# Exponentials and sines taken channel-major on half batches, with TensorE transposing the results and VectorE multiplying them from PSUM

## The chip, the cores and the metric

The kernel runs on one core of a Trainium2 chip. The metric is the device time of one execution in microseconds, as the median of several runs. An engine is named as the profile names it: PE is TensorE, DVE is VectorE, ACT is ScalarE, POOL is GpSimd, SP is the engine whose queue issues most transfers.

## The reference, cut to what matters

```python
mag = np.sqrt(a_re * a_re + a_im * a_im)
scale = np.minimum(mag, 0.999) / (mag + 1e-06)
a_re_n, a_im_n = (a_re * scale, a_im * scale)
for t in range(S):
    ar, ai = (a_re_n[:, :, t, :, None], a_im_n[:, :, t, :, None])
    new_re = ar * S_re - ai * S_im
    new_im = ar * S_im + ai * S_re
    S_re, S_im = (new_re + k_t v_t^T, new_im)
    y[:, :, t] = q_t^T S_re
```

Batch is 4, heads 8, sequence 768, head dimension 48, so that one token has 384 channels. The attention output then goes through a mixture of experts (top one of 8, 384 to 1024 to 384) and a second stage `((x @ w1) * (x @ w2)) @ w3 @ w_out`, over 3072 tokens, all in float32.

## The kernel before

**The whole.** The recurrence is computed in chunks of 128 tokens. A decay `a` is written as magnitude and angle; running sums of the log magnitude L (restarted at each chunk) and of the angle r (in turns) turn the recurrence into products: q is multiplied by exp(L/2), k by exp(-L/2), and each is taken with cos and sin of the angle. Within a chunk the scores of these products are masked and applied to v; between chunks a state S of 96 x 48 per head is carried. After the 24 chunks come the routing (which token to which expert) and the two dense stages, which are matrix products split into high and low parts.

**Two layouts.** The logs, sums and angles are worked out channel-major: 128 channels on the partitions, three tiles (index `i`) for the 384 channels, tokens along the free dimension. q and k are token-major: 128 tokens on the partitions, 384 channels along the free dimension. `f_mag` (L196) and `f_ang` (L262) do the channel-major part per batch and tile, on 128 x 768 elements, except for the first batch, which is done as two halves of 128 x 384. L and r are then brought into the token layout chunk by chunk: `t_mag` (L294) has PE transpose L into PSUM, ACT take both exponentials from there (`ep`, `em`), POOL multiply q (L304) and DVE multiply k (L305); `t_trig` (L308) does the same for r, with three activations (absolute value, sine, cosine).

**A unit** is one chunk of one batch. `t_prod` (L324) forms the four products K cos, K sin, Q cos, Q sin from SBUF operands; the table `PROD` says which of the four go to POOL (one in batch 0, two in the others), the rest go to DVE. `t_tr` (L339) transposes K and Q, four heads at a time, and copies the result out of PSUM (`kt`, `qt`); the table `EVAC` says on which engine: three of four copies on DVE in batch 0, two of four later. `t_sc` (L377) multiplies `kt` and `qt` to scores and masks them on DVE (L390). `t_y` (L394) forms the output, `t_out` (L416) transposes and stores it, `t_st1` and `t_st2` (L354, L362) update the state.

**The order of the work.** `attention` (L452) writes the program: a start (first half batch, four weight conversions `wo_conv`), then the loop over 24 units. In each unit the steps of `STEPS` are emitted in order; the products of unit i+2 are emitted at the end of unit i. Between the steps are put the preparation of the next batch, at the positions in `PLANS`, and the conversion of 20 blocks of the later weights (`w34_step`: float64 bits to float32 on DVE, L625 to L632, split on ACT and POOL, products on PE). Each engine executes its own instructions in a fixed order and waits by semaphores. ACT's functions lie in two table sets, logarithm and exponential (`setA`) and trigonometric (`setT`); a load (L172) changes between them. PSUM has eight buffers `ps`, one per result.

Of the kernel before, what the change touches and what calls it, by code (L numbers as in the profile page):

```python
# [48 lines left out]
SPAN0 = 2  # L49
# [13 lines left out]
)  # L63
ON_POOL = dict(u="110", add="010", m2="111", rat="111", turn="111", sub="111", qm="1", km="0", u0="011", add0="110", m20="011", rat0="001", turn0="000", sub0="110", qm0="1", km0="0")
STEPS = ["sc0", "kt0", "qt0", "sc1", "st1", "y0", "kt1", "lg", "qt1", "y1", "out", "st2"]
BUFS = dict(q=9, k=8, v=4, ep=3, em=2, sn=4, cs=4, Q=2, K=3, kt=4, qt=3, sts=1, S=2, pt=2, ys=3, lts=1, xr=2, st64=1, st32=3, w3h=2, w3l=1, gate=1, s1=3, s2=3, s3=2)
EXTRA = ("MAN", "OFF", "OFFP", "NR", "AIQ", "WO_A", "WO_B", "W6", "W12", "WH", "PROD", "SMUL", "EVAC", "PTE", "GATE", "ND", "D0", "M_PRE")
MAN = 0
OFF = 0
OFFP = 0  # L70
NR = '0000'
AIQ = 1
WO_A = 0
# [3 lines left out]
WH = '000'  # L77
PROD = ['0001', '0101', '1001', '0101']
SMUL = '0010'
EVAC = ['0010', '0110', '0110', '0110']  # L80
PTE = ['00', '00', '00', '00']
GATE = '01000000001100010100000010000100'
ND = 2
D0 = 19.05
M_PRE = 6
# [12 lines left out]
C_RST = C_REV + E  # L98
C_W = C_RST + S


def make_consts():
    import numpy as np

    c = np.zeros((P, C_W), np.float32)
    i = np.arange(P)
    c[:, C_ID:C_ID + P] = np.eye(P)
    c[:, C_MASK:C_MASK + P] = i[:, None] <= i[None, :]
    c[:, C_IROW:C_IROW + ROWS] = np.arange(ROWS)
    c[:, C_ICOL:C_ICOL + NCOL] = np.arange(NCOL)  # L110
    c[:, C_P1] = i - P
# [5 lines left out]
    c[:, C_RST:C_RST + S] = np.arange(S) % P != 0  # L117
# [10 lines left out]
def setup(ctx, tc, g):  # L128
# [14 lines left out]
    for i in range(NTH):  # L143
        f_load(tc, g, 0, i, 0, 1)
    g.cst = g.cp.tile([P, C_RST], F32, name="cst")
    nc.sync.dma_start(out=g.cst, in_=g.I["consts"][:, 0:C_RST])
    g.rst = g.pf.tile([P, S], F32, name="rst")
    nc.sync.dma_start(out=g.rst, in_=g.I["consts"][:, C_RST:C_W])
# [31 lines left out]
def f_load(tc, g, b, i, h0=0, h1=2):  # L180
    nc = tc.nc
    HS = S // 2
    if h0 == 0:
        g.ar[b, i] = g.pf.tile([P, S], F32, tag="ar", bufs=6, name=f"ar{b}{i}")
        g.ai[b, i] = g.pf.tile([P, S], F32, tag="ai", bufs=6, name=f"ai{b}{i}")
    sl = slice(h0 * HS, h1 * HS)
    nc.sync.dma_start(out=g.ar[b, i][:, sl], in_=g.I["are"][b, i * P:(i + 1) * P, sl])
    (nc.scalar if b == 0 and h0 == 0 and AIQ else nc.sync).dma_start(out=g.ai[b, i][:, sl], in_=g.I["aim"][b, i * P:(i + 1) * P, sl])


def eng(nc, op, b, h0, i):
    m = ON_POOL[op + "0" if b == 0 and h0 == 0 and op + "0" in ON_POOL else op]
    return nc.gpsimd if m[i:i + 1] == "1" else nc.vector


def f_mag(tc, g, b, i, h0=0, h1=2):  # L196
    nc = tc.nc
    pa = g.pf
    V, A = nc.vector, nc.scalar
    HS = S // 2  # L200
    lo, n = h0 * HS, (h1 - h0) * HS
    k = f"{b}{i}{h0}"
    ck = 2 * (2 * (b * NTH + i) + h0)
    t = {}

    def tl(nm, bufs, key):
        return pa.tile([P, S], F32, tag=nm, bufs=bufs, name=f"{key}_{k}")[:, :n]

    def o1():
        t["ar"], t["ai"] = g.ar[b, i][:, lo:lo + n], g.ai[b, i][:, lo:lo + n]  # L210
        t["s1"] = tl("s1", BUFS["s1"], "s1")
        t["s2"] = tl("s2", BUFS["s2"], "s2")
# [3 lines left out]
    def o2():  # L216
        dp = pa.tile([P, S], BF16, tag="dp", bufs=1, name=f"dp_{k}")[:, :n]
        A.activation(dp, t["ar"], AF.Relu, bias=g.hpi[:, 3:4], scale=-1.0, accum_out=g.chk[:, ck:ck + 1])
        A.activation(t["s1"], t["s1"], AF.Square, scale=0.5)
        eng(nc, "m2", b, h0, i).tensor_tensor(t["ar"], t["s1"], t["s2"], ALU.add)  # L220

    def o3():
        dp = pa.tile([P, S], BF16, tag="dp", bufs=1, name=f"dq_{k}")[:, :n]
        A.activation(dp, t["s2"], AF.Relu, bias=g.hpi[:, 2:3], accum_out=g.chk[:, ck + 1:ck + 2])

    def o4():
        tact(tc, g, t["s1"], t["s1"], AF.Ln, scale=4.0)

    def o5():
        tact(tc, g, t["s1"], t["s1"], AF.Exp, scale=-0.5)  # L230
        eng(nc, "rat", b, h0, i).tensor_tensor(t["ai"], t["ai"], t["s1"], ALU.mult)

    def o6():
        tact(tc, g, t["ar"], t["ar"], AF.Ln, scale=4.0)

    def o7():
        tact(tc, g, t["s2"], t["ar"], AF.Exp, bias=g.hpi[:, 1:2], scale=-0.5)
        V.scalar_tensor_tensor(t["s2"], t["ar"], LN999, t["s2"], ALU.min, ALU.subtract)
        V.tensor_tensor_scan(t["ar"], g.rst[:, :n], t["s2"], 0.0, ALU.mult, ALU.add)  # L239
# [66 lines left out]


def t_trig(tc, g, b, c):  # L308
    nc = tc.nc
    A = nc.scalar  # L310
    pa = g.pa
    u = f"{b}{c}"
    pr = g.ps.tile([P, 512], F32, tag="ps", name=f"pr{u}")
    for i in range(NTH):
        nc.tensor.transpose(pr[:, i * P:(i + 1) * P], g.r[b, i][:, c * P:(c + 1) * P], g.ident)
    sn = pa.tile([P, DM], F32, tag="sn", bufs=BUFS["sn"], name=f"sn{u}")
    cs = pa.tile([P, DM], F32, tag="cs", bufs=BUFS["cs"], name=f"cs{u}")
    A.activation(cs, pr[:, :DM], AF.Abs)
    tact(tc, g, sn, pr[:, :DM], AF.Sin, scale=TWO_PI)
# [987 lines left out]
```

## Time and profile before

| | us |
|---|---|
| median of 3 runs (lowest, highest) | 1011.28 (1010.45, 1015.07) |
| span of the profiled execution | 1008.9 |
| start, up to the first masked score (L390) | 0 to 56 |
| the 24 units, up to the last output | 56 to 405 |
| routing, gather and first weights | 405 to 443 |
| dense stages | 443 to 1009 |

The page gives the span of the profiled execution, from its first instruction to its last; what the runs measure has some 2.4 us around it. The mean granted clock of PE over the span is 0.923 of full speed. Busy shares over the whole span (PE 84%, DVE 57%, ACT 38%, POOL 40%) mix stages with different limits; they have to be read by stage.

### The profile page before, as it was taken

To read this page: it belongs to the slowest core of one execution; us is meant where nothing else is said; L and a number is where in the kernel's file an instruction comes from. 1 tells how busy PE (TensorE), PEld (TensorE's weight loads), DVE (VectorE), ACT (ScalarE), POOL (GpSimd) and SP (SyncE) were. 2 spreads that over 40 slices of the span, in tenths; PEclk is the share of its full clock that TensorE was granted. 3 is DMA by queue.
4 is the path that set the end of the run, shared out by engine and by line. 5 is a ranking of instruction groups with operands and counts; after the bars stand their busy time and mean duration, and the time that the engine had idled before them with its cause. 6 is when DMAs were issued, how large, how long until landed. Compare 5 with 4: busy or idle time off the path is not lost.

```text
span 1008.9 us, 14148 instructions
## 1 busy us (share of the span) xinstructions
PE 845.7 (84%) x5539; PEld 798.6 (79%) x5539; DVE 577.7 (57%) x858; ACT 378.7 (38%) x749; POOL 399.3 (40%) x295
## 2 busy tenths in 40 slices
PE   0286668776968798677999999999999999999994
PEld 0175547765857687576999999999999999999993
DVE  6998997899899999866224323224232242232221
ACT  5676557564733533323222222222222222222221
POOL 3556775777467663344016311047030172100101
PEclk9986757988887899879999999999999999999997
DMA  8445225232412443565002300014010030000000
GB/s 294 129 124 168 61 87 169 81 89 86 127 49 66 140 131 118 143 185 173 20 11 77 89 25 26 1 36 139 1 45 1 25 93 17 25 1 1 25 1 26
DMA packets 55037, 78.26 MB, mean 78 GB/s; under 512 B 15462, under 2 KB 43352, under 8 KB 54962
## 3 DMA queue, kind: packets, MB, share of 16 engines
q1 hardware_dynamic: 46322, 66.93, 21.6%
q0 software_dynamic: 5120, 9.70, 3.4%
q10 hardware_dynamic: 3520, 0.64, 0.3%
q8 instruction: 45, 0.74, 0.3%
q14 instruction: 30, 0.25, 0.1%
HBM read 64.57 MB, written 12.87 MB: 77 GB/s over the span
## 4 chain that ended last, share of the span: by engine, by line
PE 41%; DVE 26%; issue 20%; POOL 4%; DMA 3%; ACT 2%; POOLq 0%; SPq 0%; DVEq 0%; ACTq 0%
PE h L916 6%; PE o L979 6%; PE a L916 6%; PE b L916 6%; PE z L941 6%; DVE ai L272 2%; DMA wst<-in_w 2%; DVE ar L239 2%; DVE K L335 2%; DVE pt L390 2%; DVE Q L335 1%; DVE k L305 1%; PE w34p L708 1%; PE sc L383 1%; DVE cvw L627 1%
## 5 line engine op out<-in xcount | busy, mean ns | idle before, releaser
L998 POOL DMA_INDIRECT out<-osb,idx x32 | 32.2, 1005 | 350.9 <-ACT osb L995 341.8
L964 DVE TENSOR_TENSOR abt<-b,at 128x400 f32<-128x400 f32 x64 | 36.7, 574 | 169.8 <-PE b L916 165.4
L930 DVE SCALAR_TENSOR_TENSOR hl<-h,hh 128x400 fp32r<-128x400 f32 x64 | 36.6, 572 | 100.4 <-ACT hh L929 94.4
L929 ACT ACTIVATE hh<-h 128x400 fp32r<-128x400 f32 x64 | 32.1, 503 | 126.2 <-PE h L916 120.7
L967 ACT ACTIVATE abh<-abt 128x400 fp32r<-128x400 f32 x64 | 34.4, 538 | 114.2 <-DVE abt L964 107.7
L962 ACT ACTIVATE at<-a 128x400 f32<-128x400 f32 x64 | 32.3, 504 | 116.6 <-PE a L916 112.3
L968 DVE TENSOR_TENSOR abl<-abt,abh 128x400 fp32r<-128x400 f32 x64 | 51.8, 810 | 38.7 <-ACT abh L967 37.5
L941 PE MATMUL z<-hl,w2h 128*128 128x400 f32 x192 | 66.3, 345 | 5.6 <-DVE hl L930 5.6
L916 PE MATMUL h<-xl,w1h 128*128 128x400 f32 x192 | 67.3, 350 | 2.2 <-DVE xl L910 2.2
L979 PE MATMUL o<-abl,w34h 128*128 128x400 f32 x192 | 66.2, 345 | 3.0 <-DVE abl L968 3.0
L916 PE MATMUL h<-xh,w1h 128*128 128x400 f32 x192 | 67.9, 354 | 0.9 <-ACT xh L909 0.9
L916 PE MATMUL h<-xh,w1l 128*128 128x400 f32 x192 | 67.2, 350 | 0.0
L916 PE MATMUL a<-zh,m1h 128*128 128x400 f32 x192 | 66.0, 344 | 1.3 <-ACT zh L947 1.3
L941 PE MATMUL z<-hh,w2h 128*128 128x400 f32 x192 | 66.9, 349 | 0.0
L916 PE MATMUL a<-zl,m1h 128*128 128x400 f32 x192 | 66.3, 345 | 0.1
L979 PE MATMUL o<-abh,w34l 128*128 128x400 f32 x192 | 66.3, 345 | 0.0
L916 PE MATMUL b<-zh,m2l 128*128 128x400 f32 x192 | 66.1, 344 | 0.0
L916 PE MATMUL a<-zh,m1l 128*128 128x400 f32 x192 | 66.0, 344 | 0.0
L916 PE MATMUL b<-zl,m2h 128*128 128x400 f32 x192 | 65.9, 343 | 0.0
L941 PE MATMUL z<-hh,w2l 128*128 128x400 f32 x192 | 65.8, 343 | 0.0
L979 PE MATMUL o<-abh,w34h 128*128 128x400 f32 x192 | 65.7, 343 | 0.0
L916 PE MATMUL b<-zh,m2h 128*128 128x400 f32 x192 | 65.6, 342 | 0.0
(250 smaller groups left out, 2419.7 us busy)
## 6 DMA issues: line engine op xcount, KB each, us to landing
w<-in_m3t SPq DMA_DIRECT2D x16, 512.0 KB, 3.7
v<-in_v SPq DMA_DIRECT2D x24, 256.0 KB, 2.9
wst<-in_w SPq DMA_DIRECT2D x12, 512.0 KB, 3.6
wst<-in_w SPq DMA_DIRECT2D x16, 384.0 KB, 3.2
q<-in_q SPq DMA_DIRECT2D x24, 192.0 KB, 3.7
k<-in_k SPq DMA_DIRECT2D x24, 192.0 KB, 4.0
xs<-xr SPq DMA_DIRECT2D x24, 192.0 KB, 3.4
ar<-in_are SPq DMA_DIRECT2D x9, 384.0 KB, 5.1
```

The costliest lines, as they stand in the source:

```text
L239: V.tensor_tensor_scan(t["ar"], g.rst[:, :n], t["s2"], 0.0, ALU.mult, ALU.add)
L335: (tc.nc.gpsimd if PROD[b][j] == "1" else V).tensor_tensor(o, x, y, ALU.mult)
L916: TE.matmul(out, lt, rt, start=(k == 0), stop=(k == n - 1))
L929: A.activation(hh, p[:, :SUB], AF.Relu)
L930: V.scalar_tensor_tensor(hl, p[:, :SUB], 0.0, hh.bitcast(F32), ALU.max, ALU.subtract)
L941: TE.matmul(acc[s][j][:, :SUB], lt, rt, start=(f == 0 and k == 0), stop=(f == NF - 1 and k == 2))
L962: A.activation(at, pa_[:, :SUB], AF.Copy)
L964: V.tensor_tensor(t, pb_[:, :SUB], at, ALU.mult)
L967: A.activation(hi, t, AF.Copy)
L968: V.tensor_tensor(lo, t, hi.bitcast(F32), ALU.subtract)
L979: TE.matmul(acc[s][j][:, :SUB], lt, rt, start=(f == 0 and k == 0), stop=(f == NF - 1 and k == 2))
L998: G.indirect_dma_start(out=g.out if fx else g.outv[r], out_offset=bass.IndirectOffsetOnAxis(ap=idx[:, s * NRC + r:s * NRC + r + 1], axis=0 ...
```

## The change

Nothing after the attention stage is changed. In it:

- The preparation is done by half batches (three chunks), eight in all, with the three channel tiles in one tile of 128 x 1152 elements: each instruction of `f_mag` and `f_ang` handles 1152 elements, other than the running sum of the angle, which is made per channel tile (three of 384) with its carry from the half before.
- Both exponentials, the sine, the absolute value and the cosine are taken in the channel layout, on 1152 elements from SBUF, in place of 384 from PSUM per chunk. `ep`, `em`, `sn`, `cs` are then each transposed by PE, chunk by chunk (`t_tok`), and the PSUM result is multiplied directly on DVE: `t_mul` for q and k, `t_rot` for the four products. All six products of a unit are on DVE.
- All copies of `kt` and `qt` go to ACT (`EVAC`). The state's multiplication (`SMUL`) is on DVE in all batches. The magnitude, ratio, turn and subtract operations of the preparation are on POOL throughout; before, the first half batch had seven of them on DVE.
- The six products of unit i+2 become steps of unit i (`mq`, `mk`, `tc`, `ts`). q, k and v are loaded four units ahead. The preparation of half n is put at 3n - 5.2 to 3n - 2.3 units, evenly; that of the second half at 0 to 0.9. Buffers of the preparation are per half.

The core of the diff (`half` allocates a tile of 128 x 3 x 384, from a pool of its own for the last half):

```diff
-STEPS = ["sc0", "kt0", "qt0", "sc1", "st1", "y0", "kt1", "lg", "qt1", "y1", "out", "st2"]
+STEPS = ["sc0", "kt0", "mq", "qt0", "sc1", "st1", "y0", "mk", "kt1", "lg", "qt1", "tc", "y1", "out", "ts", "st2"]
-EVAC = ['0010', '0110', '0110', '0110']
+EVAC = "1111"
...
 def f_mag(tc, g, n):
...
     def o2():
...
         A.activation(t["s1"], t["s1"], AF.Square, scale=0.5)
-        eng(nc, "m2", b, h0, i).tensor_tensor(t["ar"], t["s1"], t["s2"], ALU.add)
+        G.tensor_tensor(t["ar"], t["s1"], t["s2"], ALU.add)
...
+    def o7():
...
+        g.ep[n] = half(g, n, "ep")
+        tact(tc, g, flat(g.ep[n]), t["ar"], AF.Exp, scale=0.5)
+
+    def o8():
+        tact(tc, g, t["ar"], t["ar"], AF.Exp, scale=-0.5)
+        g.em[n] = g.ar[n]
...
 def f_ang(tc, g, n):
...
+    def o2():
+        for i in range(NTH):
+            x = g.ai[n][:, i, :]
+            V.tensor_tensor_scan(x, x, x, 0.0 if n % (NCH // HC) == 0 else g.carry[:, i:i + 1], ALU.add, ALU.bypass)
+        g.sn[n] = half(g, n, "sn")
+        t["sn"] = flat(g.sn[n])
+        V.tensor_scalar(t["sn"], t["ai"], MAGIC, MAGIC, ALU.add, ALU.subtract)
+    def o3():
+        G.tensor_tensor(t["ai"], t["ai"], t["sn"], ALU.subtract)
...
+    def o4():
+        tact(tc, g, t["sn"], t["ai"], AF.Sin, scale=TWO_PI)
+        A.activation(t["ai"], t["ai"], AF.Abs)
+    def o5():
+        tact(tc, g, t["ai"], t["ai"], AF.Sin, bias=g.hpi[:, 0:1], scale=-TWO_PI)
+        g.cs[n] = g.ai[n]
...
+def t_tok(tc, g, src, u, nm):
+    b, c = u
+    n, k = divmod(b * NCH + c, HC)
+    p = g.ps.tile([P, 512], F32, tag="ps", name=f"{nm}{b}{c}")
     for i in range(NTH):
+        tc.nc.tensor.transpose(p[:, i * P:(i + 1) * P], src[n][:, i, k * P:(k + 1) * P], g.ident)
+    return p[:, :DM]
+def t_mul(tc, g, u, which):
+    p = t_tok(tc, g, g.ep if which == "q" else g.em, u, "p" + which)
+    x = (g.q if which == "q" else g.k)[u]
+    tc.nc.vector.tensor_tensor(x, x, p, ALU.mult)
+def t_rot(tc, g, u, a):
...
+    p = t_tok(tc, g, g.sn if a else g.cs, u, "sc"[a]).rearrange("p (h d) -> p h d", h=H)
+    for o, x in ((g.K, g.k), (g.Q, g.q)):
+        V.tensor_tensor(o[u][:, :, a, :], x[u].rearrange("p (h d) -> p h d", h=H), p, ALU.mult)
...
+        put([setA] + mag1 + [setT] + f_ang(tc, g, 1), 0.0, 0.9)
+        for hb in range(2, NHB):
+            x = HC * hb - 5.2
+            pre, mag = f_mag(tc, g, hb)
+            if hb + 1 < NHB:
+                put([lambda hb=hb: f_load(tc, g, hb + 1)], x, x)
+            put(pre, x, x + 0.7)
+            put([setA] + mag + [setT] + f_ang(tc, g, hb), x + 0.7, x + 2.9)
+        for i in range(LEAD, n):
+            put([lambda i=i: t_load(tc, g, *units[i])], i - LEAD + 0.3, 0)
```

## Rows read from the trace of the kernel before

**Rows 1.** Stretches: busy us (instructions) by engine, PE clock, DMA, GB/s.

```profile
0.00:56.00 56.00, 12.06 (x60) 9.17 (x61) 45.42 (x70) 36.56 (x86) 27.10 (x35) 1.00 0.68 225
56.00:405.00 349.00, 270.63 (x2317) 235.21 (x2314) 324.20 (x408) 188.96 (x368) 225.41 (x142) 0.82 0.34 103
353.46:398.99 45.53, 43.12 (x459) 38.43 (x458) 44.91 (x76) 17.73 (x37) 23.15 (x16) 1.00 0.38 122
443.00:1008.90 565.90, 540.99 (x3044) 535.44 (x3042) 180.73 (x315) 141.05 (x276) 131.64 (x106) 0.99 0.14 40
```

**Rows 2.** Groups of DVE, 0 to 410 us: shapes, count, busy us, mean ns.

```profile
L305 DVE TENSOR_TENSOR k<-k,em 128x384 f32<-128x384 f32 x24 | 24.5, 1036 | 0.0
...
L335 DVE TENSOR_TENSOR Q<-q,cs 128x384 f32<-128x384 f32 x24 | 21.2, 885 | 0.0
L348 DVE COPY tk<-tpk 96x512 f32<-96x512 f32 x30 | 20.2, 675 | 0.5 <-PE tpk L345 0.4
...
L335 DVE TENSOR_TENSOR K<-k,cs 128x384 f32<-128x384 f32 x18 | 17.6, 979 | 1.7 <-ACT cs L166 1.2 <-PE tpk L345 0.5
...
L348 DVE COPY tq<-tpq 96x512 f32<-96x512 f32 x24 | 16.2, 674 | 0.0
...
L335 DVE TENSOR_TENSOR K<-k,sn 128x384 f32<-128x384 f32 x12 | 10.4, 868 | 1.7 <-ACT sn L166 1.7
```

**Rows 3.** Single lines of DVE: shortest, median, longest duration in ns.

```profile
L372 DVE TENSOR_TENSOR S<-sp,S x16: 540/543/556, 59.3 to 392.6; 96x384 f32<-96x384 f32 x16
...
L335 DVE TENSOR_TENSOR Q<-q,cs x24: 540/666/2158, 48.9 to 389.1; 128x384 f32<-128x384 f32 x24
...
L627 DVE SCALAR_TENSOR_TENSOR cvw<-w,cvw x16: 674/1002/1559, 149.8 to 383.5; 128x512 uint32<-128x512 uint32 x16
...
L239 DVE TENSOR_TENSOR_SCAN ar<-rst,s x15: 924/1740/9291, 25.6 to 286.5; 128x768 f32<-128x768 f32 x9, 128x384 f32<-128x384 f32 x6
```

**Rows 4.** Timeline of DVE and POOL from 272 us: start, duration in us.

```profile
272.15 9.29 DVE L239 TENSOR_TENSOR_SCAN ar<-rst,s 128x768 f32<-128x768 f32 x1
...
273.53 1.00 POOL L335 TENSOR_TENSOR Q<-q,sn 128x384 f32<-128x384 f32 x1
274.49 5.33 POOL L231 TENSOR_TENSOR ai<-ai,s 128x768 f32<-128x768 f32 x3
```

**Rows 5.** Groups of POOL, 0 to 405 us.

```profile
L335 POOL TENSOR_TENSOR Q<-q,sn 128x384 f32<-128x384 f32 x24 | 31.5, 1312 | 10.0 <-PE tpq L345 9.0 <-DMA q<-in_q 1.0
L304 POOL TENSOR_TENSOR q<-q,ep 128x384 f32<-128x384 f32 x24 | 31.4, 1326 | 14.3 <-ACT ep L166 14.3
...
L335 POOL TENSOR_TENSOR K<-k,sn 128x384 f32<-128x384 f32 x12 | 20.5, 1708 | 19.4 <-PE lq L448 14.2 <-PE tpk L345 5.2
...
L335 POOL TENSOR_TENSOR K<-k,cs 128x384 f32<-128x384 f32 x6 | 9.9, 1655 | 17.0 <-ACT sn L166 10.3 <-PE tpk L345 6.3 <-PE lq L448 0.5
```

**Rows 6.** Groups of ACT, 0 to 410 us.

```profile
L166 ACT ACTIVATE s<-s 128x768 f32<-128x768 f32 x18 | 14.3, 835 | 0.0
...
L350 ACT ACTIVATE tq<-tpq 96x512 f32<-96x512 f32 x24 | 14.1, 588 | 19.7 <-PE tpq L345 19.6
L172 ACT ACT_TABLE_LOAD x10 | 12.8, 1283 | 2.3 <-issue 2.2
```

**Rows 7.** Timeline: chain start, cosine of unit 0, first mask, last output.

```profile
7.22 0.52 ACT L213 ACTIVATE s<-ai 128x384 f32<-128x384 f32 x1 [1.48 <-DMA ai<-in_aim]
...
47.11 0.62 ACT L166 ACTIVATE cs<-cs,hpi 128x384 f32<-128x384 f32 x1
...
56.05 0.69 DVE L390 TENSOR_TENSOR pt<-sc,cst 128x512 f32<-128x512 f32 x1 [0.41 <-PE sc L383]
...
404.80 0.60 ACT L412 ACTIVATE ys<-yT 128x512 f32<-128x512 f32 x1 [4.34 <-PE yT L409]
```

**Rows 8.** Group of PE, 50 to 400 us: transposes of L.

```profile
L298 PE MATMUL pl<-cst,ar 128*128 128x128 f32 x63 | 13.8, 336 | 10.8 <-DVE ar L239 6.1 <-DVE tk L348 2.8 <-DVE pt L390 2.0
```

**Rows 9.** Longest wait of ACT, 56 to 405 us: total us, times, longest.

```profile
ACT ec L166 <- DVE ar L239: 24.7, 10, 5.9
```

More of the change, by code (lines that the diff above doesn't have):

```diff
@@ L48 @@
 AMIN = 0.75
-SPAN0 = 2
+HC = 3
+HS = HC * P
+NHB = B * NCH // HC
 W_PRE = 1
@@ L142, in setup @@
     g.pf = g.pfx.enter_context(tc.tile_pool(name="pf", bufs=1, side="right"))
[L143 to L148, printed above, removed]
+    f_load(tc, g, 0)
+    g.cst = g.cp.tile([P, C_W], F32, name="cst")
+    nc.sync.dma_start(out=g.cst, in_=g.I["consts"])
+    g.rst = g.pf.tile([P, NTH * HS], F32, name="rst")
+    nc.gpsimd.memset(g.rst, 1.0)
+    nc.gpsimd.memset(g.rst[:, ::P], 0.0)
     g.ident = g.cst[:, C_ID:C_ID + P]
@@ L177, in table_set, with half, f_load, f_mag @@
     g.aset, g.aops = i, []
-def f_load(tc, g, b, i, h0=0, h1=2):
+def half(g, n, nm):
+    pool, bufs = (g.pl, 1) if n == NHB - 1 else (g.pf, BUFS[nm])
+    return pool.tile([P, NTH, HS], F32, tag=nm, bufs=bufs, name=f"{nm}{n}")
+def f_load(tc, g, n):
     nc = tc.nc
[L182 to L196, printed above, removed]
-    nc = tc.nc
[L198 to L203, printed above, removed]
+    b, h = divmod(n, NCH // HC)
+    g.ar[n], g.ai[n] = half(g, n, "ar"), half(g, n, "ai")
+    pieces = [slice(i, i + 1) for i in range(NTH)] if n == 0 else [slice(0, NTH)]
+    for x in pieces:
+        for t, nm, q in ((g.ai[n], "aim", nc.scalar if n == 0 else nc.sync), (g.ar[n], "are", nc.sync)):
+            q.dma_start(out=t[:, x, :], in_=g.I[nm][b].rearrange("(i p) s -> p i s", p=P)[:, x, h * HS:(h + 1) * HS])
+def f_mag(tc, g, n):
+    nc = tc.nc
+    pf = g.pf
+    V, A, G = nc.vector, nc.scalar, nc.gpsimd
     t = {}
-    def tl(nm, bufs, key):
-        return pa.tile([P, S], F32, tag=nm, bufs=bufs, name=f"{key}_{k}")[:, :n]
+    def tl(nm, dt=F32, key=None):
+        return pf.tile([P, NTH * HS], dt, tag=nm, bufs=BUFS.get(nm, 1), name=f"{key or nm}_{n}")
+    def flat(x):
+        return x.rearrange("p i s -> p (i s)")
     def o1():
-        t["ar"], t["ai"] = g.ar[b, i][:, lo:lo + n], g.ai[b, i][:, lo:lo + n]
-        t["s1"] = tl("s1", BUFS["s1"], "s1")
-        t["s2"] = tl("s2", BUFS["s2"], "s2")
+        t["ar"], t["ai"] = flat(g.ar[n]), flat(g.ai[n])
+        t["s1"], t["s2"] = tl("s1"), tl("s2")
         A.activation(t["s2"], t["ai"], AF.Square, scale=0.5)
@@ new lines, in o6 @@
+    def o6():
+        tact(tc, g, t["s1"], t["s1"], AF.Exp, scale=-0.5)
+        G.tensor_tensor(t["ai"], t["ai"], t["s1"], ALU.mult)
+    def o7():
+        b, h = divmod(n, NCH // HC)
+        cs = slice(h * HC, (h + 1) * HC)
+        if h == 0:
+            g.ec[b] = g.cp.tile([P, NTH, NCH], F32, tag="ec", bufs=2, name=f"ec{b}")
+            g.ecb[b] = g.cp.tile([2 * D, H, NCH], F32, tag="ecb", bufs=2, name=f"ecb{b}")
+        ec, ecb = g.ec[b], g.ecb[b]
+        tact(tc, g, ec[:, :, cs], g.ar[n][:, :, P - 1::P], AF.Exp, scale=0.5)
+        nc.sync.dma_start(out=g.ecd[b].rearrange("(i p) c -> p i c", p=P)[:, :, cs], in_=ec[:, :, cs])
+        for h2 in range(2):
+            nc.sync.dma_start(out=ecb[h2 * D:(h2 + 1) * D, :, cs], in_=g.ecd[b].rearrange("(h d) c -> d h c", d=D)[:, :, cs])
+        g.ep[n] = half(g, n, "ep")
+        tact(tc, g, flat(g.ep[n]), t["ar"], AF.Exp, scale=0.5)
@@ L308, in t_trig @@
[L308 to L319, printed above, removed]
-    tact(tc, g, cs, cs, AF.Sin, bias=g.hpi[:, 0:1], scale=-TWO_PI)
-    g.sn[b, c], g.cs[b, c] = sn, cs
@@ L456, in attention @@
     g.pw = pwx.enter_context(tc.tile_pool(name="pw", bufs=1, side="right"))
-    with tc.manual_schedule(engines=g.manual) if MAN else ExitStack(), tc.tile_pool(name="psA", bufs=8, space=PSUM) as ps, ExitStack() as pax:
+    with tc.tile_pool(name="psA", bufs=8, space=PSUM) as ps, ExitStack() as pax:
         g.ps = ps
         g.aset, g.aops = None, []
-        for nm in "L r ecb q k v S Q K kt qt pt ys sn cs s lts w3f w3 ec wo64 w364".split():
+        for nm in "ep em sn cs ecb ec q k v S Q K kt qt pt ys lts w3f w3 wo64 w364".split():
             setattr(g, nm, {})
@@ L504, in attention @@
             wo_load(tc, g, m)
-        for f in hB["load"]:
-            f()
-        ops = hA["pre"] + hA["mag"]
-        wo = 0
-        for x, f in enumerate(ops):
-            f()
-            while wo < min(NWO, (x + 1 - WO_A) * NWO / WO_B):
+        f_load(tc, g, 1)
+        pre, mag = f_mag(tc, g, 0)
+        wo = 0
+        for x, f in enumerate(pre + mag):
+            f()
+            while wo < min(NWO, (x + 1) * NWO / 8):
                 wo_conv(tc, g, wo)
                 wo += 1
-        for wo in range(wo, NWO):
-            wo_conv(tc, g, wo)
         pwx.close()
+        g.pl = pax.enter_context(tc.tile_pool(name="pl", bufs=1, reuse_waits="tile"))
         g.pa = pax.enter_context(tc.tile_pool(name="pa", bufs=1, reuse_waits="tile"))
-        for f in hA["tl"] + hB["pre"][:F1] + hA["tm"] + [hA["ec"], setT] + hA["ang"] + hB["pre"][F1:] + hA["trig"]:
-            f()
+        for u in units[:LEAD]:
+            t_load(tc, g, *u)
+        setT()
+        for f in f_ang(tc, g, 0):
+            f()
+        f_load(tc, g, 2)
+        pre1, mag1 = f_mag(tc, g, 1)
+        for f in pre1:
+            f()
+        jit = dict(mq=lambda u: t_mul(tc, g, u, "q"), mk=lambda u: t_mul(tc, g, u, "k"), tc=lambda u: t_rot(tc, g, u, 0), ts=lambda u: t_rot(tc, g, u, 1))
         for u in units[:2]:
-            t_prod(tc, g, *u)
+            for nm in ("mq", "mk", "tc", "ts"):
+                jit[nm](u)
         for hf in range(2):
@@ L538, in wgoal, with put @@
             return wd + (x - D0) * (wtot - wd) / (n - W_END - D0)
-        queue, cur = [], hB
-        def plan(x0, cur, nxt, T):
-            q = []
-            def put(ops, lo, hi):
-                for j, f in enumerate(ops):
-                    q.append((x0 + lo + (hi - lo) * j / max(1, len(ops)), f))
-            if nxt:
-                put(nxt["load"], T[0], T[1])
-                put(nxt["pre"][:W_F], T[8], T[9])
-                put(nxt["pre"][W_F:], T[10], T[11])
-            if cur:
-                put([setA] + cur["mag"], T[0], T[1])
-                put(cur["tl"], T[2] - LEAD, T[3] - LEAD)
-                put(cur["tm"], T[2], T[3])
-                put([cur["ec"]], T[4], T[4])
-                put([setT] + cur["ang"], T[6], T[7])
-                put(cur["trig"], T[10], T[11])
-            q.sort(key=lambda t: t[0])
-            return q
+        queue = []
+        def put(ops, lo, hi):
+            for j, f in enumerate(ops):
+                queue.append((lo + (hi - lo) * j / max(1, len(ops)), f))
+        put([setA] + mag1 + [setT] + f_ang(tc, g, 1), 0.0, 0.9)
[8 more added lines that the diff above has]
+            put([lambda i=i: t_load(tc, g, *units[i])], i - LEAD + 0.3, 0)
+        queue.sort(key=lambda t: t[0])
         for i in range(n):
             b, c = units[i]
-            if i in (0, SPAN0) or (c == 0 and b > 0):
-                assert not queue
-                nxt = prep(1 if i == 0 else 2 if i == SPAN0 else b + 2)
-                queue = plan(i, cur, nxt, PLANS[0 if i == 0 else 1 if i == SPAN0 else 2 if nxt else 3])
-                cur = nxt
             has = i + 1 < n
@@ L580, in attention @@
                         steps.append(lambda w=nm[0], h=int(nm[2]): t_tr(tc, g, b1, c1, h, w))
+                elif nm in jit:
+                    if i + 2 < n:
+                        steps.append(lambda nm=nm: jit[nm](units[i + 2]))
                 elif nm == "lg":
@@ L589, in attention @@
             for j, f in enumerate(steps):
-                with hp(OFF):
-                    f()
+                f()
                 x = i + (j + 1) / len(steps)
@@ L596, in attention @@
                     queue.pop(0)[1]()
-            if b == B - 1 and c == 0:
+            if i == n - NCH:
                 g.pfx.close()
@@ L602, in attention @@
                 g.w3d = [g.pm.tile([P, NTH * FF], R, tag="m2" + x, name="w3d" + x) for x in "hl"]
-            if i + 2 < n:
-                with hp(OFFP):
-                    t_prod(tc, g, *units[i + 2])
             if b == B - 1:
```

143 lines of the change are left out of this document (30 added, 113 removed), and 4 rows, old and new, of the table PLANS.

## The prediction

> **What bounds the kernel now.** I read the stretches first. The dense stages, 443 to 1009 us, keep PE busy for 541.0 of 565.9 us at a granted clock of 0.99 [rows 1]; the change does not touch them, and they begin when the attention stage and the routing are done. So the change is worth what it moves the end of the 24 units, now at 405 us [rows 7]. [...] DVE is the bound there: shorter DVE work is a shorter stage as long as PE and ACT keep feeding it.
>
> Then I asked what DVE's time is made of. A product of 128 x 384 on DVE with both operands in SBUF takes 540 ns at its shortest but 0.87 to 1.04 us on average [rows 2, 3]; an addition of the same width with one operand in PSUM takes 540 to 556 ns, always [rows 3]. The difference is POOL: a scan whose median is 1.74 us took 9.29 us while POOL worked back to back; it ended at 281.4 us, 1.6 us, or its own length, after the last of POOL's three products [rows 3, 4]. So DVE instructions that read only SBUF are held up by POOL, those that read PSUM are not. The 78 products on DVE took 24.5 + 21.2 + 17.6 + 10.4 = 73.7 us [rows 2] where 78 x 0.54 = 42 would do.
>
> **The change, part by part, on DVE.** (1) Products: 78 go, 73.7 us. In their place come 6 x 24 = 144 with one PSUM operand; the addition's 0.545 us is the nearest row [rows 3], so 78.5 us: +4.8. Bounds: 144 x 0.54 and 144 x 0.556, or 1 us either way. (2) The copies of kt and qt leave DVE: 54 of them, 20.2 + 16.2 = -36.4 us [rows 2]. (3) The state's multiplication of batch 2 comes back from POOL, four instructions of about 1 us as the other SBUF products [rows 2]: +4. (4) The seven operations of the first half batch that go to POOL, 4 to 5 us, lie ahead of the units, where DVE does not set the end: 0. (5) Whole-half instructions handle the same elements: 0; a running sum of 384 costs 0.92 us at its shortest against 1.74 for 768 [rows 3], so cutting it finer adds about 0.1 us each for nine more, and the others lose as many starts. (6) What stays and reads only SBUF, some 190 of the 408 instructions in the units (conversions, logs, sums), is held up less or more. Now a conversion loses 1.00 - 0.67 = 0.33 us at the median [rows 3], the products lost 0.4; 190 x 0.33 = 62 us in all. POOL gives up 66 products, 31.5 + 31.4 + 20.5 + 9.9 = 93.3 of its 252.5 us, or 37% [rows 1, 5]. That alone would take 23 us off. Against it, POOL's remaining instructions grow: 384 elements take 1.00 us and 768 take 5.33 / 3 = 1.78 [rows 4], so 1152 take about 2.56, and whoever meets one waits longer. If the hold-ups grew by a fifth it would cost +12. I take -10, nearer to the load than to the length, and keep -23 and +12 as ends. Sum: 4.8 - 36.4 + 4 - 10 = -37.6, of which some 4 us lie ahead of 56 us: -34, ends -47 and -12. DVE in the units: 324 - 34 = 290 us.
>
> [...]
>
> **On the other engines.** PE gets 144 transposes more; 63 took 13.8 us [rows 8], so +32 us at the present clock, 302 in all. At full clock it is (270.6 x 0.82) + 26 = 248. In 353 to 399 us PE was busy 95% and its clock stood at 1.00 [rows 1], so I expect the clock to rise with the load; PE stays just behind DVE. ACT gets the 54 copies at 0.59 us = 32, and six more table loads (16 for 10) at 1.28 = 8 [rows 6]; the channel-major activations save a few starts: about 224 us in the units. POOL falls to 225 - 93 - 6 = 126. The transfers are the same bytes in halves, put three units ahead on SP's queue, q, k and v four units ahead; behind them there stands the store of a unit's output, which nothing in the units waits for: 0.
>
> **New waits.** Each DVE product now waits for three transposes, and holds one of the eight PSUM buffers until it is done; behind it on DVE stand the next mask and state update, behind the transposes on PE the next scores. They are put two units ahead, a unit being 349 / 24 = 14.5 us, so this wait costs nothing unless PE itself is late. PE is late when ACT is: every `kt` and `qt` now stands in ACT's queue behind whole-half activations, which take up to 1.5 x 0.835 = 1.25 us [rows 6], and behind ACT's own waits for scans and POOL. For that I let DVE's busy share drop from 93% to 91%: 290 / 0.91 = 319 us, against 349: -30. Ends: 0.93 and 0.88.
>
> **The start.** Now the chain runs from the last piece of the angle data, 7.22 us, to the first mask, 56.05 [rows 7]. After: twelve activations of at most 1.25 us (15.0), four POOL operations of 2.56 (10.2), on DVE two sums (2.6 + 2.8), two combined operations of at most 1152 / 512 x 0.67 = 1.5 and a rounding (1.5), one table load (1.3), and from the last cosine to the first mask what it is now, 56.05 - 47.11 = 8.9: 7.2 + 15.0 + 10.2 + 9.9 + 1.3 + 8.9 = 52.5; what can overlap (two activations, POOL's ratio beside the exponentials) takes up to 5 off. I take 49: -7. The weight conversions fill DVE's gaps there.
>
> **Sum.** The span is 1008.9 us, and 2.4 us of the median of 1011.3 lie around it. 1011.3 - 30 - 7 = 974. The forecast's own range goes from DVE at -47 with 93% busy (277 / 0.93 = 298: -51 -9 = 951) to DVE at -12 with 93% (336: -13 -4, 994) or, with -34, 88% (330: -19 -4, 988); I stretch it to 1000 for both at once in part.
>
> **Rivals.** *A, the hold-ups are kept.* POOL's fewer but longer instructions hold DVE as long in all as now, so that dropping 78 products saves only their 42 us: 78.5 - 42 - 36.4 + 4 = +4, and with the start 1011.3 + 4 - 7 = 1008. For it: the 9.29 us scan, where POOL's instructions came back to back [rows 4], and those of 1152 elements are as long as three. Against: POOL's load falls by 37%. *B, ACT's queue, slower.* In a half, ACT needs results of others four times: the sum of squares (2.56), the scan (1.5 + 2.6), the ratio (2.56), and the angle through POOL, three sums, rounding and POOL (2.56 + 2.8 + 1.5 + 2.56): 18 us, more with hold-ups. ACT has room for (349 - 224) / 7 = 18 us of standing still per half in the units. If little fills these waits and hold-ups make them 23 us, the stage takes 224 + 7 x 23 = 385: +36 - 7, 1040. It decides from 18 us per half on. For it: ACT waits longest already for a scan, 24.7 us in ten waits, 5.9 the longest [rows 9], and now the copies stand behind. Against: the steps of a half are spread over 2.2 units, 30 us, with copies between. *C, more relief.* Hold-ups fall faster than POOL's load, as its instructions now come singly: 62 less 35, DVE 265 us; PE at full clock then is 248 and near, so 93%: 285, and 1011.3 - 64 - 7 = 940. That the change fails to do what it says can be left out: the copies and products are fixed to their engines by the lines shown.
>
> **Chances.** Forecast 0.60, A 0.13, B 0.17, C 0.10. Faster by over 0.5% (5 us, what a measurement here can tell from none) is the forecast and C: 0.70; A is 0.13 for the same; B 0.17. The range takes the forecast, A and the near parts of B and C, 945 to 1022; beyond lie half of C and most of B, some 0.2.
>
> **What would show it.** Right: in the units DVE near 290 us and the busiest; the six products at 0.54 to 0.56 us with no spread; no DVE copy of kt or qt; POOL near 126 us; the first mask near 49 us; PE's clock above 0.82; the dense stages as long as now. Wrong: conversions and scans with medians above those of now (A); ACT's waits for DVE and POOL above 120 us, with PE waiting for ACT's copies and the clock falling (B); a first mask later than 56 us; DVE below 85% busy, whatever the cause.

## The result, and the profile after

The kernel after takes 982.15 us at the median of four runs (981.2 to 985.78), the one before 1011.69 beside it: a ratio of 0.9713, 95% interval 0.9686 to 0.974, so 29.5 us less. The forecast was 974, the range 945 to 1022. The profiled execution took 985.78 us, with a span of 984.0. It was the longest of its four, so the two profiles differ by 24.9 us (spans 1008.9 and 984.0) where the medians differ by 29.5.

The stretches of the kernel after: start, units, routing, dense stages (columns as in [rows 1]: length in us, busy us and instructions of PE, PEld, DVE, ACT and POOL, PE's clock, DMA share, GB/s).

```profile
0.00:57.00 57.00, 10.70 (x67) 9.83 (x67) 36.73 (x53) 32.64 (x36) 22.73 (x27) 1.00 0.64 201
57.00:379.00 322.00, 272.06 (x2458) 243.36 (x2456) 283.24 (x424) 210.95 (x315) 114.42 (x63) 0.87 0.39 114
379.00:417.00 38.00, 21.99 (x131) 19.25 (x129) 22.64 (x62) 12.45 (x21) 15.78 (x12) 0.78 0.74 189
417.00:984.00 567.00, 542.83 (x3032) 537.83 (x3032) 180.48 (x315) 140.24 (x274) 132.03 (x106) 0.98 0.14 40
```

The units take 322 us in place of 349 [rows 1], and that is the gain in the profile: the stages behind them are as long as before (605 us for 604), and the start is not shorter (57 us for 56). In the units DVE has 283 us for 324, POOL 114 for 225, ACT 211 for 189, and PE's clock is 0.87 for 0.82. DVE's share has fallen from 93% (324.2 of 349.0 us, [rows 1]) to 88%.

Single lines of DVE in the kernel after: shortest, median, longest in ns, over the whole span. They answer to [rows 3].

```profile
L309 DVE TENSOR_TENSOR K<-k,s x24: 528/548/555, 49.0 to 364.0; 128x384 f32<-128x384 f32 x24
...
L298 DVE TENSOR_TENSOR k<-k,pk x24: 522/546/555, 40.4 to 362.9; 128x384 f32<-128x384 f32 x24
...
L573 DVE SCALAR_TENSOR_TENSOR cvw<-w,cvw x16: 675/693/2653, 123.9 to 346.9; 128x512 uint32<-128x512 uint32 x16
...
L209 DVE TENSOR_TENSOR_SCAN ar<-rst,s x8: 2542/4006/4956, 22.9 to 300.4; 128x1152 f32<-128x1152 f32 x8
```

The products from PSUM have no spread, as forecast. The conversions' median is down from 1002 to 693 ns: of the 16 in the row, nine run beside no POOL instruction, and the four that take 1.64 to 2.65 us begin beside one. But the scan over a half, 2.54 us at its shortest, takes 4.0 at the median, so it is held 1.5 us, where the scan of 768 elements before was seldom held (seven of nine took within 0.02 us of the shortest, 1.72); that half of the prediction's sign of rival A is there.

The start of the kernel after, from the timelines of DVE, POOL and ACT (start, duration in us). L208 is the combined operation ahead of the scan L209, L213 POOL's ratio, L252 the three running sums of the angle, L191 and L197 the second half's square and sum of squares, the last line the first half's cosine.

```profile
20.21 1.65 DVE L208 SCALAR_TENSOR_TENSOR s<-ar,s 128x1152 f32<-128x1152 f32 x1
21.79 1.15 DVE L578 TENSOR_SCALAR wo<-wo 128x384 uint32<-128x384 uint32 x1
22.85 4.96 DVE L209 TENSOR_TENSOR_SCAN ar<-rst,s 128x1152 f32<-128x1152 f32 x1
...
35.99 4.51 DVE L252 TENSOR_TENSOR_SCAN ai<-ai 128x384 f32<-128x384 f32 x3
...
22.68 2.72 POOL L213 TENSOR_TENSOR ai<-ai,s 128x1152 f32<-128x1152 f32 x1
...
35.37 2.62 POOL L197 TENSOR_TENSOR ar<-s,s 128x1152 f32<-128x1152 f32 x1
...
16.42 1.24 ACT L147 ACTIVATE s<-ar,hpi 128x1152 f32<-128x1152 f32 x1
...
29.02 1.15 ACT L191 ACTIVATE s<-ai 128x1152 f32<-128x1152 f32 x1
...
46.79 1.25 ACT L147 ACTIVATE ai<-ai,hpi 128x1152 f32<-128x1152 f32 x1
```

L208's input is ready at 17.66 us (16.42 + 1.24) and L208 begins at 20.21, behind weight conversions; one more conversion stands between it and the scan. The scan lies beside the ratio and takes 4.96 us, the sums lie beside the second half's sum and take 4.51. The last cosine ends at 48.0 us, the first mask begins at 57.0.

### The profile page after: what moved, and what is told of

It reads as the page before. It is cut to its first block, busy times and chain, and to the rows that moved or that the text cites. A ratio compares the mean times of both kernels' runs of the same rounds, so it can differ in the third digit from the quotient of the medians.

```text
span 984.0 us, 14181 instructions
## 1 busy us (share of the span) xinstructions
PE 847.6 (86%) x5683; PEld 810.3 (82%) x5683; DVE 523.1 (53%) x852; ACT 396.3 (40%) x645; POOL 285.0 (29%) x206
## 4 chain that ended last, share of the span: by engine, by line
PE 46%; issue 21%; DVE 19%; DMA 5%; POOL 4%; ACT 3%; SPq 0%; POOLq 0%; ACTq 0%; DVEq 0%
PE h L863 7%; PE a L863 6%; PE b L863 6%; PE o L926 6%; PE z L888 6%; DVE ar L209 2%; PE sc L356 2%; DVE ai L252 2%; DMA wst<-in_w 2%; PE tpk L318 2%; PE yT L373 2%; PE tpq L318 1%; PE sp L332 1%; DVE cvw L573 1%; PE yT L378 1%
```

## The experiments

All times of the experiments stand beside runs of the kernel before on the same chip (medians 1010.0 to 1010.9); the kernel after was timed beside others (1011.7), so experiments are best compared with it by the ratios. "Held" is worked out from single DVE instructions: each one's duration less the shortest that its form (operation and shapes) has in any of these runs, summed over the units; groups (line, tiles and form) with a mean excess under 0.04 us, almost all of those that read PSUM among them, are left out. "Units" go from the first mask to the start of the last output's copy (321 us in the kernel after, for the stretch of 322 above). First mask, units, DVE, POOL and held are from the one profiled execution of each kernel.

| kernel | median us | ratio to before (95%) | first mask | units us | DVE | POOL | held |
|---|---|---|---|---|---|---|---|
| before | 1011.7 | | 56.0 | 349 | 324 | 225 | 101 |
| e2 before, copies on ACT | 1012.7 | 1.0034 (1.0015-1.0053) | 55.1 | 349 | 300 | 216 | 104 |
| e6 before, products on DVE | 1001.1 | 0.9930 (0.9902-0.9958) | 55.9 | 339 | 314 | 153 | 64 |
| e7 before, both | 993.0 | 0.9835 (0.9800-0.9870) | 56.4 | 332 | 292 | 148 | 69 |
| after | 982.15 | 0.9713 (0.9686-0.9740) | 57.0 | 321 | 283 | 114 | 52 |
| e11 one copy back | 983.8 | 0.9733 (0.9702-0.9764) | 55.4 | 322 | 293 | 116 | 51 |
| e1 two copies back | 996.1 | 0.9866 (0.9835-0.9898) | 55.8 | 323 | 294 | 121 | 38 |
| e3 products from SBUF | (other data) | | 56.3 | 313 | 288 | 134 | 67 |
| e5 idle load, ahead of the turn too | 1026.4 | 1.0173 (1.0129-1.0217) | 80.2 | 341 | 288 | 150 | 58 |
| e5b idle load on POOL | 998.1 | 0.9899 (0.9846-0.9952) | 55.8 | 336 | 303 | 202 | 73 |
| e4 POOL in thirds | 968.1 | 0.9587 (0.9556-0.9619) | 55.8 | 305 | 273 | 137 | 43 |
| e8 start cleared | 978.4 | 0.9692 (0.9664-0.9720) | 54.0 | 321 | 281 | 115 | 49 |
| e10 start on DVE | 972.8 | 0.9629 (0.9604-0.9654) | 49.1 | 316 | 283 | 116 | 52 |
| e12 e4 and e10 | 960.95 | 0.9511 (0.9485-0.9537) | 47.1 | 308 | 272 | 136 | 40 |

### What the copies are worth: e1, e11, e2

```diff
-EVAC = "1111"
+EVAC = "0110"     (e1; e11: "1110")
```

> The kernel after, with two of a unit's four copies of kt and qt (48 of 96) back on DVE. Theory, DVE bounds the units: 48 x 0.67 = 32 us come back to DVE, 283 + 32 = 315, at 88 to 90% busy 350 to 358 us for the units in place of 322: the time near 1010 to 1018, and the start as long as now. Rival, ACT's queue bounds the units by now (its copies stand behind its waits): ACT falls from 211 to about 183, PE and DVE get their kt and qt earlier, DVE's share goes up to 95%, units at most 332, the time 982 to 992.

> The kernel after, with one of a unit's four copies (qt of the second four heads, 24 in all, 16 us) back on DVE. Two copies back gave +14 us at the median with ACT 22 us less busy. Theory, both engines feed each other and DVE is the nearer bound: +3 to +10, the time 985 to 992. Rival, ACT's queue is the nearer one and the best split lies between: -2 to -6, the time 976 to 980.

Two copies back cost 14 us at the median, one copy 1.6, which is inside the intervals. Neither reading of e1 held, nor of e11: it was no 28 us or more, and ACT, at 189 us, was not what held the units. The profiled execution of e1 took 984.7 us with a mean PE clock of 0.950; its other four took 995.1 to 997.6 at 0.933 to 0.939. So its units of 323 us don't show where the 14 us went; the lower clock goes with them, but whether as cause or consequence stays open. What the profile does show: 46 copies, 31 us, came to DVE in the units and its busy time rose by 11 only, since held fell by 14; these copies read PSUM.

```diff
-EVAC = ['0010', '0110', '0110', '0110']
+EVAC = ['1111', '1111', '1111', '1111']     (in the kernel before)
```

> The kernel before, with all 96 copies of kt and qt on ACT (54 move), and nothing else. Theory, DVE bounds the units: 324 - 36 = 288 us on DVE, at 91 to 93% 310 to 316 in place of 349, the time near 975; the mean times of conversions, sums and of the products from SBUF stay as they are, with POOL near 225. Rival, the units hold together only with the rest of the change: ACT at 189 + 32 = 221 and POOL's products late, DVE below 87% busy, the time above 995.

The rival held, and this is the run that says most against the prediction. 54 copies leave DVE, DVE falls by 24 us to 86%, and the units stay at 349. The windows of that run over the units, and four stretches in them:

```profile
55.00:405.00 350.00, 264.38 (x2311) 227.36 (x2310) 299.89 (x357) 213.52 (x425) 216.34 (x143) 0.85 0.33 104
...
213.70:238.30 24.60, 14.13 (x127) 11.37 (x123) 24.50 (x20) 15.00 (x31) 20.39 (x11) 0.87 0.15 49
238.30:252.90 14.60, 13.08 (x100) 12.16 (x102) 11.19 (x17) 9.97 (x22) 6.13 (x5) 0.74 0.55 173
252.90:275.00 22.10, 19.70 (x179) 17.51 (x180) 17.14 (x25) 16.97 (x27) 7.40 (x6) 0.88 0.40 125
275.00:300.00 25.00, 18.77 (x124) 15.99 (x123) 23.39 (x20) 9.36 (x22) 19.39 (x12) 0.77 0.18 56
```

For 24.6 us POOL works on the preparation and on weight splits (20.4 busy) and DVE is busy all the time with 20 instructions, 1.2 us each, of which 12.0 us in all are held; PE has 10 us free. Then POOL is done, PE makes up its backlog (13.1 of 14.6 us, at a clock of 0.74) and DVE has 3.4 us to spare, and 5.0 in the next stretch; from 275 on it is nearly full again (23.4 of 25.0) beside POOL (19.4). In these 86 us the held time comes in such blocks, and what the copies left free lies between them.

### POOL's products: e6, e7

```diff
-PROD = ['0001', '0101', '1001', '0101']
+PROD = ['0000', '0000', '0000', '0000']     (and the q products too; e7: with the EVAC of e2)
```

> The kernel before, with its 66 products off POOL and on DVE, from SBUF as they were; copies and all else as before. Theory 1, what DVE has to do sets the units: 324 + 66 x 0.54 = 360, less 37% of its 62 us of hold-ups (23) = 337 us, at 93% busy 362 in place of 349, the time near 1024. Theory 2, POOL's queue, in which products, ratios and subtractions wait for each other's givers, sets the units together with DVE: units at most 349, the time 995 to 1012, with DVE's share up.

> The kernel before, with all copies of kt and qt on ACT and all products on DVE from SBUF: the change without its channel-major factors, its half batches and its PSUM sources. Theory 2 (POOL's queue and DVE held the units together, so that the copies alone gave nothing and both together give most): DVE 300 + 36 - 23 = 313 us, at 91 to 95% busy 330 to 344, the time 990 to 1005; what is left to 982 is the worth of PSUM and channel-major. Rival: the gain is in the channel-major factors alone (fewer ACT instructions, earlier factors): the time within 5 us of 1011.

In e6 DVE gets 66 products more, 61 of them in the units, and its busy time *falls* from 324 to 314 us: 61 x 0.54 = 33 us of work came and 38 us of held time went (the last 5 us are overlap: DVE instructions that follow one another at once overlap by 0.08 us at the median in the profiles of before and after, and 61 x 0.08 = 5). The time falls by 9 us (1010.0 to 1001.1). With the copies on ACT as well (e7) it is 993.0, 8 us less again, where the copies alone had given nothing. So the times are those of theory 2 in both runs, though DVE's share in e6 did not go up (92 for 93%): POOL's products were what the units waited for. That they did so mostly by way of DVE is read from the waits of PE in the kernel before (PEld is its weight load), not tested by itself:

```profile
PE tpk L345 <- DVE K L335: 13.9, 4, 6.4
PE tpq L345 <- DVE Q L335: 8.0, 3, 3.2
...
PEld tpq L345 <- POOL K L335: 3.5, 1, 3.5
```

What is left from e7 to the kernel after, 11 us (12 by the ratios), is the worth of the rest of the change together: the channel-major halves, the PSUM sources, and the new order of steps and loads. No run here takes those apart; held falls by 17 us between the two kernels (69 to 52).

### Held by POOL: e3, e5, e5b, e4

```diff
-    return p[:, :DM]
+    return src[n][:, k, :]     (t_tok: an SBUF slice of the same tile; the transposes stay)
```

> The kernel after, whose 144 products on DVE take their factor from SBUF (384 neighbouring elements of the same channel-major tile) and not from PSUM; the transposes are made all the same, but nobody reads them, so the factors of q and k are other numbers. Theory, a PSUM source keeps a product clear of POOL: shortest 540 ns as now, mean 0.70 to 0.80 in place of 0.545, +25 to +35 us on DVE, and the time +15 to +30 (a little is gained as the products no longer wait for PE). Rival 1, POOL at 114 us seldom meets them: mean within 0.60, the time within 5 us. [...]

Other factors send other tokens to the experts, so the dense stages are longer (761 us); the units alone can be compared. Single lines of DVE in e3:

```profile
L309 DVE TENSOR_TENSOR K<-k,sn x24: 543/550/2529, 46.0 to 341.0; 128x384 f32<-128x384 f32 x24
...
L298 DVE TENSOR_TENSOR k<-k,ar x24: 528/546/2966, 40.5 to 310.7; 128x384 f32<-128x384 f32 x24
```

Its units, by engine:

```profile
56.30:369.00 312.70, 255.92 (x2454) 227.20 (x2452) 288.04 (x416) 206.04 (x314) 133.86 (x62) 0.93 0.39 119
```

The products from SBUF are held again, up to 2.97 us, with the same shortest time as from PSUM (528 to 543 ns against 521 to 539). In the units the six groups took 102.7 us in place of 71.8, +31, as the theory had it. But held rose by 15 only, and DVE as a whole by 5: the other instructions were held less (the scans 18.9 us for 25.5, the conversions L573 and L574 22.7 for 32.6), and eight instructions fewer fall in the shorter units. So of the 31 us that the products are spared by reading PSUM, 16 lie on other instructions. And the units became 9 us *shorter*, against the expectation: DVE's idle time in them fell by 14 us (39 to 25). The waits of DVE in the units of the kernel after (total, times, longest) that e3 cannot have:

```profile
DVE k L298 <- PE pk L291: 5.6, 6, 2.7
...
DVE K L309 <- PE s L291: 2.6, 4, 1.0
...
DVE K L309 <- PE c L291: 2.3, 3, 1.3
...
DVE q L298 <- PE pq L291: 1.5, 3, 0.8
```

Together they are 12.0 us, and in e3, at 92% busy, they are gone. PE's clock was higher too (0.93 for 0.87); no run separates the two.

At the longest, a product took 2.97 us from SBUF (e3) and 0.555 from PSUM (the kernel after).

Next came load put back on POOL, first badly:

```diff
+    if b < B - 1:
+        tc.nc.gpsimd.tensor_tensor(g.dmy, g.rst[:, :DM], g.rst[:, DM:2 * DM], ALU.mult)     (e5, in t_tok)
...
+    if 2 <= u[0] * NCH + u[1] < 18:
+        for _ in range(2):
+            tc.nc.gpsimd.tensor_tensor(g.dmy, x, g.rst[:, :DM], ALU.mult)     (e5b, in t_mul, x the product)
```

> The kernel after, with 72 idle products of 128 x 384 put on POOL, one beside each transpose group of the units' factors in the first three batches; nobody reads them. Theory, hold-ups go with POOL's load: POOL 114 to some 190 us, the SBUF-only instructions of DVE are held 39 x 190 / 114 = 65 us in place of 39, DVE near 309, the time +20 to +30; products from PSUM stay at 0.545. Rival, hold-ups go with the length of POOL's single instructions: those of 384 elements hold nobody for long, DVE within 8 us of 283, the time within 8 us of 982.

e5 took 1026.4 us, but not for the reason under test: its idle products depend on nothing, so 24 of them stood in POOL's queue ahead of the first half's turn, which began at 56.05 us in place of 34.26, and the first mask came at 80.2 us. Its units are 20 us longer as well, with DVE only 5 us busier and held up by 6; what else made them longer is open. The run decides nothing about holding.

> The kernel after, with 64 idle products of 128 x 384 on POOL, each reading a q or k that DVE has just multiplied (units 3 to 18, four each), so that they are spread over the units; nobody reads them. Theory, POOL's load holds DVE: some 0.3 us of DVE for each us of POOL, as before (60 of 225) and after (39 of 114): POOL near 180, DVE 283 + 20 = 303, units +12 to +25, the time 994 to 1007, with the first mask at 57 as now. Rival, it is POOL's own queue that costs (angles and sums of squares behind the load): DVE within 6 us of 283 but idle longer before what POOL gives. Rival 2, neither: the time within 6 us of 982.

The units of e5b, by engine:

```profile
56.00:393.00 337.00, 276.32 (x2461) 247.08 (x2463) 303.27 (x423) 210.76 (x316) 201.74 (x127) 0.87 0.37 109
```

The theory held, to the microsecond on DVE (303), and DVE was not idle longer (34 us for 39), as POOL's own queue would have made it. POOL got 87 us more, held rose by 21, DVE by 20, the units by 15. The price was lower than forecast for each POOL microsecond, 21 / 87 = 0.24, where the kernel before has 101 / 225 = 0.45 and the one after 52 / 114 = 0.46 (the expectation counted less held time, 60 and 39 us). These were instructions of 384 elements. Is it their length?

```diff
-        G.tensor_tensor(t["ar"], t["s1"], t["s2"], ALU.add)
+        for i in range(NTH):
+            x = slice(i * HS, (i + 1) * HS)
+            G.tensor_tensor(t["ar"][:, x], t["s1"][:, x], t["s2"][:, x], ALU.add)     (ratio and subtraction likewise)
```

> The kernel after, with each of POOL's three whole-half operations of 128 x 1152 (sum of squares, ratio, subtraction) cut into three of 128 x 384. Rival A of the prediction, hold-ups go with the length of POOL's single instructions: the held time of DVE falls by a third or more, DVE 283 to below 270, units 10 to 15 us shorter, the time near 970. Theory, hold-ups go with the time that POOL works, however it is cut: DVE within 6 us of 283, POOL a little up, the time within 5 us of 982.

The units of e4, by engine:

```profile
56.00:361.00 305.00, 257.12 (x2455) 230.52 (x2454) 273.04 (x423) 209.43 (x315) 136.59 (x103) 0.93 0.40 120
```

The scan in the same run:

```profile
L211 DVE TENSOR_TENSOR_SCAN ar<-rst,s x8: 2753/2988/3355, 22.6 to 284.2; 128x1152 f32<-128x1152 f32 x8
```

My theory fell, and rival A came near. The same work in thirds makes POOL *busier* by 22 us, and yet the time falls by 14, to 968.1. The scan's median goes from 4.01 to 2.99 us and its longest from 4.96 to 3.36; held falls to 43, DVE by 10, and DVE's idle time in the units by 7 (322 - 283 = 39, 305 - 273 = 32). So length counts beside load, as the prediction's rival A said: 43 / 137 = 0.31 per POOL microsecond. It is less than "a third or more" of the held time, though (52 to 43). PE's clock in the units rose too, from 0.87 to 0.93. In e1 and e11, whose windows follow, it was 0.90 and 0.89 and the units as long as in the kernel after; that speaks against the clock as the cause, but those two also gave DVE 10 us more to do:

```profile
56.00:379.00 323.00, 263.98 (x2454) 233.77 (x2453) 294.05 (x468) 188.59 (x268) 121.44 (x62) 0.90 0.38 113
55.00:378.00 323.00, 270.77 (x2463) 242.16 (x2461) 293.29 (x446) 200.53 (x292) 116.44 (x62) 0.89 0.38 114
```

### The start: e8, e10

```diff
-            while wo < min(NWO, (x + 1) * NWO / 8):
+            while wo < (1 if x < 7 else NWO):
...
+            AFTER.update({f"wo{m}": i.ins for m in range(1, NWO)})     (i: the first half's scan)
+            AFTER["pre", 1] = i     (i: the first half's last cosine)
```

> The kernel after, with three of four early weight conversions put behind the first half's scan on DVE, and the second half's preparation behind the first half's cosine on ACT; the same work in another order. Theory, the start lost its expected 7 us to what stands between the steps of the first half: scan from 19 us, last cosine near 40 in place of 48, first mask 48 to 50 in place of 57, the time 6 to 9 us less, near 974. Rival, the chain's own instructions and POOL's hold-ups make the 57, or conversions ahead of the sums take it back: first mask 54 or later, the time within 3 us of 982.

The scan began at 19.1 us, as expected, but took 4.78 beside the ratio; the turn then waited for POOL's weight splits until 32.0. First mask 54.0, the time 3.8 us less at the median (runs of 976.1 to 980.6 against 981.2 to 985.8, though the intervals of the two ratios overlap). That is nearer to the rival (54 or later) than to the theory's 48 to 50.

```diff
-        G.tensor_tensor(t["ai"], t["ai"], t["s1"], ALU.mult)
+        i = (G if n else V).tensor_tensor(t["ai"], t["ai"], t["s1"], ALU.mult)     (on top of e8; sum of squares, turn, subtraction likewise)
```

> The kernel of the cleared start, with the four POOL operations of the first half (sum of squares, ratio, turn, subtraction) on DVE; nothing else moves. Theory, what was left of the long start are POOL's operations at 2.6 to 2.8 us for 1.35 on DVE, the scan held beside the ratio (4.8 for 2.5 us) and the weight splits ahead of the turn (3.2): last cosine near 36 in place of 42.8, first mask 46 to 48 in place of 54, the time 6 to 8 us below that kernel's 978, near 971. Rival, the units are paced by what the second half and the loads give: the first mask comes earlier and the end does not, the time 976 to 980.

The scan, the ratio and the cosine of the first half in the timelines of e10:

```profile
18.32 2.56 DVE L218 TENSOR_TENSOR_SCAN ar<-rst,s 128x1152 f32<-128x1152 f32 x1
20.80 1.33 DVE L224 TENSOR_TENSOR ai<-ai,s 128x1152 f32<-128x1152 f32 x1
...
37.91 1.25 ACT L155 ACTIVATE ai<-ai,hpi 128x1152 f32<-128x1152 f32 x1
```

With the ratio on DVE behind it, the scan takes 2.56 us. The cosine ends at 39.2, the first mask comes at 49.1, and the time is 972.8, 5.6 us below e8 and 9.4 below the kernel after. All that the earlier start gives (4.9 and 7.9 us at the first mask) arrives at the end. Two things are in it: the scan no longer runs beside the ratio, and the four operations are shorter on DVE (the ratio 1.33 us for 2.72).

### Both: e12

> The kernel after, with POOL's three operations of each half cut into thirds (that alone gave 968.1, 14 less) and the cleared start whose first half has its sums of squares, ratio, turn and subtraction on DVE (that alone gave 972.8, 9 less). Theory, the two lie in different stretches, the units and the start, and add up: first mask 46 to 50, units 302 to 308, the time 957 to 963. Rival, both shorten the same wait of the units for the halves: no better than the thirds alone, 966 to 970.

The edit is e4's and e10's together. 960.95 us (957.2 to 963.4), the first mask at 47.1, units of 308: the two add up but for 2 us (21.2 below the kernel after, of 14.1 + 9.4 = 23.5). This version beats both kernels, at 0.9511 of the one before. Its start and its units, by engine:

```profile
0.00:47.00 47.00, 9.94 (x65) 9.09 (x66) 33.81 (x54) 27.12 (x31) 16.93 (x24) 1.00 0.74 235
47.00:356.00 309.00, 260.99 (x2459) 234.19 (x2457) 271.63 (x426) 213.95 (x321) 136.42 (x103) 0.91 0.40 120
```

## Why the prediction was right, and where not

The time was within the range and 8 us above the forecast. In the profiled execution, 985.8, 8 us are the start, 3 the units (322 for 319) and 1 the dense stages. The units' term, -27 for -30, came out for reasons that were in part others than its own: it gave nearly all of the gain to the copies, and alone they gave none (e2). That the sum was so near is partly luck.

**The start** was the term that failed: -7 forecast, +1 measured. The step summed the chain's own durations and said that conversions "fill DVE's gaps there". They did more. The combined operation ahead of the scan began 2.6 us after its input was ready (20.21 for 17.66) and one conversion more, 1.2 us, stood ahead of the scan; the scan took 2.4 us more than its shortest beside POOL's ratio (4.96), and the sums of the angle 1.7 more than theirs (4.51) beside the second half's sum: 8 us together. Moving the conversions and the second half's preparation out of the way gave 3 of them back (e8, 54.0). e10 has its first mask at 49.1, but that it meets the step's 49 is chance: the step had POOL's four operations at 2.56 us each, and e10 has them on DVE, the ratio at 1.33.

**The products** (1) were right: 543 to 547 ns at the mean, 144 of them, 78.4 us. Nothing shows that a source in SBUF would have been cheaper: before, the shortest product from SBUF and the shortest addition from PSUM took 540 ns each [rows 3], and the shortest products 528 to 543 ns from SBUF in e3 and 521 to 539 from PSUM in the kernel after.

**The copies** (2) left DVE as counted. But that they shorten the units was wrong as an argument by itself: moved alone they gave +2 us (e2), moved after POOL's products -8 (e6 to e7). In the kernel after, one of four moved back costs nothing that can be told (e11).

**The hold-ups** (6) were mis-sized. I took 190 x 0.33 = 62 us and -10. Before, 101 us were held in the units, of which 30 lay on the products there; the other 71 became 52, -19, nearer to the end of -23 that followed POOL's load. Hence DVE at 283 and not 290.

**"DVE is the bound"** was half of it. 93% busy was true, but nearly a third of that time was DVE being held (101 us): 24 us less on DVE changed nothing (e2), 66 products more on DVE made the units shorter (e6).

**New waits** were put at nothing "unless PE itself is late". They are 12.0 us on DVE, and without them DVE is 92% busy (e3); this, with the share taken at 91% and found at 88%, gave back what DVE had gained beyond the forecast. ACT at 211 us (forecast 224) and POOL at 114 (126) came out lower than said; PE's clock above 0.82 and dense stages of the same length came as said.

**Rivals.** A as a whole fell, since held time halved, but the length of POOL's instructions, which it rests on, counted in e4: cut into thirds they held DVE 43 us for 52, and the time fell by 14. B fell: ACT with one or two copies fewer made nothing faster (e11, e1), and ACT's waits for DVE and POOL, 120 us or more by B, are 52 in the units (the longest group 19.6). Of C's 35 us of relief 19 came.

## What to carry to other kernels

In these kernels part of DVE's busy time was waiting for POOL (held 101 of 324 us before, 52 of 283 after): compare the mean of a group with its shortest, and before moving work off the busy engine, lighten the one that holds it (e6) or cut its long instructions (e4). Test a bound by taking away work from it alone; 93% busy was not proof (e2). In a chain at the start of a kernel, count also what is placed between its steps and what runs beside them.

## What the runs showed of the hardware

Three instructions of 384 elements on POOL in place of one of 1152 held DVE less (43 us for 52, e4) although POOL was busy longer in all (137 us for 114). Holding did not simply add up: with the 144 products back in SBUF (e3) they took 31 us more in the units, but held rose by 15 and DVE by 5. The copies out of PSUM were in part free: 31 us of them came to DVE in e1 and it was busy 11 us longer. And holding went both ways: with the products in SBUF (e3), POOL's own busy time rose from 114 to 134 us with the same 62 or 63 instructions.
